# Two of the first four row tiles loaded on the ScalarE DMA queue instead of the SyncE queue

## The chip, the cores and the metric

The kernel runs on one core of one Trainium2 chip. The metric is the device time of one execution in microseconds (us). A profile covers the span of one execution, which is about 1.8 us shorter than the timed value (831.1 against 832.94 us for the changed kernel). The granted clock is the share of its full clock that TensorE was given; its mean over a run is 1.00 unless a number is stated.

Some names that recur: TensorE does matmuls (PE in the profile) and loads their weights (PEld). VectorE is DVE, ScalarE is ACT, GpSimd is POOL. In this kernel SyncE (SP) does nothing but issue transfers. A `q` after an engine's name (SPq, ACTq) means its instruction sequencer, which also issues transfers. Both SyncE and ScalarE issue loads here, each on a queue of its own (q1 and q10 in the profiles: 9.48 and 0.53 MB in the first 30 us of the changed kernel).

## The reference, cut to what matters

One transformer block: a layernorm with modulation, linear attention, a residual, a second layernorm, a gated feed-forward part. Only its beginning matters here:

```python
x = A_x                                            # 2048 x 1024, bfloat16
mod = (_silu(c) @ w_mod).reshape(c.shape[0], 6, 1, -1)
sa, ca, ga, sb, cb, gb = ...                       # six rows of 1024
h = _layernorm(x, axis=-1) * (1 + ca) + sa
q, k, v = split(h @ wqkv)                          # attention follows
```

The rows of `x` are taken in 16 tiles of 128 rows; four tiles make a chunk of 512 rows. Apart from one small transpose of `c`, TensorE can do nothing that the result needs before the first tiles have been loaded, normalized and transposed.

## The kernel before: the parts that the change touches

The kernel writes down all operations of all engines in one order; each engine executes its own in that order, and a wait is inserted wherever one operation needs another's result. The transfers at the start (cut):

```python
P.dma("c", CS8[0:NDT, :], cv8, queue="act")              # ScalarE queue
for st in range(4):                                       # row tiles 0..3, 256 KB each
    P.dma("x0_%d" % st, XRES[:, st, :], xv[:, st, :])     # SyncE queue
ca_load(0)            # w_mod, 1 MB, rows of 1 KB      (first weight load)
wq_load(0, 2)         # wqkv, 512 KB, rows of 2 KB
ca_load(1); wq_load(2, 2); ...                            # more weights, in order of use
```

The layernorm of the first chunk (cut; `dve`, `act`, `pe`, `pool` say which engine):

```python
warm(13, bank=3)                # PE: matmuls on zeros, to fill the time
act_stats(1)                    # ACT: mean and variance of tile 1, two passes
for f in s0_: f()               # DVE: statistics of tile 0
ln1_rstd1(0)                    # DVE + POOL: rstd, the scale of tile 0
s2_[0](); s2_[1]()              # DVE: statistics of tile 2
act_xn(0, MV[:, 0, 0:1])        # DVE: shift of tile 0 (nmr); ACT: normalizes tile 0
tile_transposes(0)              # PE: 8 transposes of tile 0
warm(5, bank=3)                 # PE
act_var(1)                      # DVE: from ACT's sums of tile 1
s2_[2]() ...                    # DVE, POOL: rstd of tiles 1 and 2
s3_[0](); s3_[1](); s3_[2]()    # DVE: statistics of tile 3
ln1_rstd1(3)
act_xn(1, SUMX[:, 1:2])         # DVE, ACT: normalizes tile 1
ln1_xn(2)                       # DVE: normalizes tile 2
tile_transposes(2)              # PE: 8 transposes of tile 2
mod_sc(WCA, 8, range(2))        # PE: first use of the first weight load
ln1_xn(3)                       # DVE: normalizes tile 3
tile_transposes(1, 3)           # PE
```

ScalarE normalizes tile 0 only after its own two passes over tile 1.

## Time and profile before

| | before |
|---|---|
| time, median of 6 runs (lowest to highest) | 831.07 us (830.88 to 831.25) |
| TensorE busy | 824.0 of 829.4 us |
| last landing event of tiles 0, 1, 2, 3 | 3.62, 4.25, 5.92, 6.58 us |
| first transposes (tile 0), then those of tile 2 | 8.76, 10.29 us |

A landing event is an increment of a load's semaphore in the trace; each of these loads has 16, and whoever waits for the load goes on after the last (tile 2's last comes at 5.92, and VectorE, which waits for it, starts at 5.94).

First the head of the page of the kernel before:

```profile
span 829.4 us, 10017 instructions
PE 824.0 (99%) x4083; PEld 378.4 (46%) x4083; DVE 312.0 (38%) x665; ACT 197.6 (24%) x336; POOL 39.8 (5%) x57
```

TensorE is busy nearly all the time, so only what delays TensorE counts. The chain that ended last, in order of time (columns: start, duration, what):

```profile
1.71 4.21 DMA xres<-in_A_x_dram
5.92 0.02 issue
5.94 1.29 DVE stats L176 x2
...
7.47 1.23 ACT xres L176
8.71 0.05 issue
8.76 818.08 PE ps L176 x4069
```

It reads: the load of tile 2 lands at 5.92, VectorE takes its statistics, then tile 0's shift; ScalarE normalizes tile 0; from 8.76 us to the end TensorE never waits. What happens on VectorE and on TensorE in between, from the timeline of the kernel before (start, duration, engine, source line, operation, output<-input, and in brackets the idle time before it and what ended that):

```profile
5.94 1.29 DVE L176 BATCH_NORM_STATS2 stats<-xres 128x6 f32<-128x512 bf16 x2 [0.58 <-DMA xres<-in_A_x_dram]
7.14 0.20 DVE L176 TENSOR_SCALAR nmr<-mv,rstd 128x1 f32<-128x1 f32 x1
7.88 1.27 DVE L176 BATCH_NORM_STATS2 stats<-xres 128x6 f32<-128x512 bf16 x2
9.62 1.18 DVE L176 TENSOR_SCALAR xres<-xres,mv,rstd 128x1024 bf16<-128x1024 bf16 x2
...
8.76 0.62 PE L176 MATMUL ps<-ident,xres 128*128 128x128 bf16 x8 [0.42 <-ACT xres L176]
9.21 1.24 PE L176 MATMUL ps<-e,ident 128*128 128x512 bf16 x5
10.29 0.61 PE L176 MATMUL ps<-ident,xres 128*128 128x128 bf16 x8
```

The statistics at 5.94 are tile 2's, those at 7.88 are tile 3's, and the normalization at 9.62 is tile 2's (its partner in the same line is tile 3's). On TensorE five fill matmuls stand between the transposes of tile 0 and those of tile 2. They are done at about 10.3 (matmuls overlap at their ends, so 9.21 + 1.24 reaches past 10.29), just after VectorE has finished the first half of its 1.18 us, tile 2 (about 10.2): the join is tight but without a wait.

### The profile page before, as it was taken

What the parts mean: (1) busy time and instruction counts of PE and PEld (TensorE: products, weight loads), DVE (VectorE), ACT (ScalarE), POOL (GpSimd) and SP (SyncE); (2) the same over time, 40 slices, a digit from 0 to 9 for tenths busy, and PEclk for the clock granted to TensorE, in tenths of its full rate; (3) what the DMA queues carried; (4) which work ended last, traced back from release to release, by engine and by line L of the source; (5) the groups of instructions that cost most, each with busy time, mean ns of one, the idle gap of its engine ahead of it and who ended that gap; (6) DMA issues with size and microseconds to landing.
All of it is one profiled execution on the core that took longest, in us unless ns stands there. A gap on an engine that the chain in (4) does not pass through costs nothing.

```text
span 829.4 us, 10017 instructions
## 1 busy us (share of the span) xinstructions
PE 824.0 (99%) x4083; PEld 378.4 (46%) x4083; DVE 312.0 (38%) x665; ACT 197.6 (24%) x336; POOL 39.8 (5%) x57
## 2 busy tenths in 40 slices
PE   8999999999999999999999999999999999999998
PEld 4544444454444444444444444444444444444444
DVE  5797986756955521121221111122111111221111
ACT  4757641323242111011111101111110111111011
POOL 1010000000130000030000003000000300000000
PEclk9999999999999999999999999999999999999999
DMA  9969655928397996700455570045557004553000
GB/s 320 288 151 229 149 159 172 202 102 304 60 258 225 259 267 174 192 25 14 128 150 155 150 188 28 15 126 153 153 153 187 26 18 125 154 151 86 0 26 26
DMA packets 199245, 119.28 MB, mean 144 GB/s; under 512 B 57880, under 2 KB 182944, under 8 KB 199200
## 3 DMA queue, kind: packets, MB, share of 16 engines
q1 hardware_dynamic: 199184, 118.65, 52.7%
q8 instruction: 32, 0.52, 0.3%
q14 instruction: 13, 0.11, 0.0%
q10 hardware_dynamic: 16, 0.00, 0.0%
HBM read 100.67 MB, written 4.33 MB: 127 GB/s over the span
## 4 chain that ended last, share of the span: by engine, by line
PE 99%; DMA 1%; DVE 0%; ACT 0%; SPq 0%; issue 0%
PE ps L176 99%; DMA xres<-in_A_x_dram 1%; DVE stats L176 0%; ACT xres L176 0%; SPq L176 0%; DVE xres L176 0%; DVE mv L176 0%; DVE nmr L176 0%
## 5 line engine op out<-in xcount | busy, mean ns | idle before, releaser
L176 PE MATMUL ps<-h2t,gug 128*128 128x512 bf16 x896 | 211.7, 379 | 0.0
L176 PE MATMUL ps<-h2t,guu 128*128 128x512 bf16 x896 | 211.7, 379 | 0.0
L176 DVE TENSOR_TENSOR at<-sg,ps 128x512 bf16<-128x512 bf16 x112 | 77.1, 688 | 282.7 <-PE ps L176 281.1
L176 ACT ACTIVATE sg<-ps 128x512 bf16<-128x512 f32 x112 | 66.9, 597 | 309.7 <-PE ps L176 309.7
L176 PEld LDWEIGHTS ps<-h2t,guu 128*128 128x128 bf16 x896 | 87.5, 98 | 105.8
L176 PEld LDWEIGHTS ps<-h2t,gug 128*128 128x128 bf16 x896 | 87.4, 98 | 105.7
L176 PE MATMUL ps<-wd_a,at 128*128 128x512 bf16 (+1 forms) x512 | 112.4, 378 | 0.0
L176 PE MATMUL ps<-ht,wqk 128*128 128x512 bf16 x512 | 111.7, 379 | 0.0
L176 PE MATMUL ps<-wd_b,at 128*128 128x512 bf16 (+1 forms) x384 | 85.0, 378 | 0.0
L176 PEld LDWEIGHTS ps<-wd_a,at 128*128 128x128 bf16 x512 | 50.0, 98 | 59.8
L176 DVE TENSOR_TENSOR ut<-att,gb_b 128x512 bf16<-128x512 bf16 (+1 forms) x32 | 13.8, 430 | 167.5 <-ACT att L176 167.5
L176 PEld LDWEIGHTS ps<-ht,wqk 128*128 128x128 bf16 x512 | 49.4, 98 | 58.8
L176 ACT ACTIVATE att<-ps 128x512 bf16<-128x512 f32 (+1 forms) x32 | 17.4, 591 | 182.1 <-PE ps L176 182.1
L176 PEld LDWEIGHTS ps<-wd_b,at 128*128 128x128 bf16 x384 | 37.5, 98 | 44.7
L176 PE MATMUL ps<-pk,xres 128*128 128x512 bf16 x256 | 56.5, 379 | 0.0
L176 PE MATMUL ps<-mw,pqt 128*128 128x512 bf16 x256 | 56.3, 379 | 0.0
L176 POOL TENSOR_SCALAR h2t<-h2t,modcol 128x512 bf16<-128x512 bf16 x32 | 26.4, 841 | 383.0 <-DMA h2t<-xn 383.0
L176 ACT ACTIVATE e<-ps 128x512 bf16<-128x512 f32 x56 | 33.1, 603 | 31.7 <-PE ps L176 20.5
L176 PEld LDWEIGHTS ps<-mw,pqt 128*128 128x128 bf16 x256 | 24.8, 98 | 30.3 <-DVE xres L176 0.4
L176 PEld LDWEIGHTS ps<-pk,xres 128*128 128x128 bf16 x256 | 24.8, 98 | 30.0 <-issue 0.4
L176 ACT ACTIVATE junk<-xres 128x1024 bf16<-128x1024 bf16 x24 | 25.4, 1058 | 35.1 <-DVE xres L176 34.9
L176 DVE SCALAR_TENSOR_TENSOR xres<-ps,xres 128x512 bf16<-128x512 f32 x32 | 21.4, 689 | 12.3 <-PE ps L176 11.7
(107 smaller groups left out, 346.0 us busy)
## 6 DMA issues: line engine op xcount, KB each, us to landing
gug<-in_B_w_gate_dram SPq DMA_DIRECT2D x56, 512.0 KB, 3.9
guu<-in_B_w_up_dram SPq DMA_DIRECT2D x56, 512.0 KB, 5.2
xres<-in_A_x_dram SPq DMA_DIRECT2D x20, 256.0 KB, 7.8
rb<-recip_den SPq DMA_DIRECT2D x8, 512.0 KB, 11.5
stgx<-in_w_mod_dram SPq DMA_DIRECT2D x2, 2048.0 KB, 7.8
wd_a<-in_B_w_down_dram SPq DMA_DIRECT2D x4, 1024.0 KB, 7.8
out_dram<-xres SPq DMA_DIRECT2D x31, 128.0 KB, 1.7
xres<-in_A_x_dram SPq DMA_DIRECT2D x3, 1024.0 KB, 14.0
```

What stands on the lines that cost most here:

```text
L176: return getattr(e, method)(**kw)
```

## The change

Its intent is to issue the four loads from two engines, so that the tiles are issued sooner and the weights behind them too.

```diff
         for st in range(4):
-            P.dma("x0_%d" % st, XRES[:, st, :], xv[:, st, :])
+            P.dma("x0_%d" % st, XRES[:, st, :], xv[:, st, :], queue="act" if st % 2 else "sp")
```

## The prediction

> **What bounds the kernel.** The page's first part has TensorE busy 824.0 of 829.4 us (99%). The chain of waits puts one unbroken run of 4,069 matmuls from 8.76 us to the end, 818.08 us; the waits view shows no matmul wait after 8.76 us. The granted clock is 1.00. So only the start of the first real transposes (8.76 us) moves the time, one for one, unless a later load comes late.
>
> The chain before 8.76 us (timeline): SyncE issues the row tiles at 0.79, 1.25, 1.71 and 2.18 us (0.40 to 0.43 us each). Their last landing events are at 3.62, 4.25, 5.92 and 6.58 us. VectorE takes tile 0's statistics at 3.64, waits for tile 2 (0.58 us idle), takes its statistics 5.94 to 7.22, and only then, in order, makes tile 0's shift (7.14 to 7.34). ScalarE normalizes tile 0 at 7.46 (1.24 us); TensorE follows at 8.76. So tile 2's landing sets the start.
>
> **What the change removes, adds, moves.** No work is added or removed.
> - Two issues leave SyncE: tile 2 is issued at about 1.25 instead of 1.71 us, the weight loads behind it 0.93 us sooner.
> - ScalarE gets two issues (about 0.43 us each) behind its load of c (0.79 to 1.37). Tile 1 is issued at about 1.40 (before: 1.25), tile 3 at about 1.86 (before: 2.18). ScalarE's table load moves from 1.40 to about 2.33, so SiLU of c ends near 3.8 and VectorE's copy of it near 4.0. Tile 0's statistics stand behind that copy: near 4.0 instead of 3.64.
> - [...] 365 and 389 GB/s from 2.5 to 3.5 us already. [...] Then tile 0 lands near 3.9, tile 1 near 4.5, tile 2 between 5.4 and 6.3, tile 3 near 6.7. No trace here shows two loaded queues yet.
>
> **Sum.** If tile 2 lands by 5.7, VectorE does 4.0 + 1.3 + 0.4 and goes on without a wait; transposes start near 8.55 (gain 0.2 us). If sharing holds tile 2 to 6.2, they start near 9.05 (loss 0.3 us). ScalarE's statistics of tile 1 (2.3 us) end by 6.9. The first weight load (landed 10.45, used 10.74) ends behind the same bytes and should hardly move. Expected: 831.2 us, 8 in 10 between 830.6 and 831.8. Faster by over 2% 0.003, within 2% 0.99, slower by over 2% 0.007.
>
> **What would show each step.** Timeline: ScalarE's three issues in a row, the table load near 2.33, tile 0's statistics near 4.0; idle of VectorE before tile 2's statistics tells whether sharing or VectorE binds. The chain: matmuls from 8.5 to 9.1 us, still about 818 us long. DMA view: two data queues, same bytes.
>
> **What would make it wrong.** With uneven sharing tile 2 could land near 5.0 or wait behind tiles 1 and 3 (loss up to 0.7 us). If the first weight loads are held back past their use near 10.7 or 12.4 us, TensorE stalls within the run of matmuls. [...] (first weight tile: median landing 8.78, last 10.45); if that lag changes, so do the landings.

## The result, and the profile after

The changed kernel took 832.32 us (median of 6 runs, 831.32 to 834.99) against 831.07. The ratio is 1.0019, with a 95% interval of 1.0005 to 1.0033. Ratios here are the mean time of one kernel's fast runs over that of the other's in the same rounds, so not quite the ratio of the medians. The class "within 2%" was right, which says little about a change of this size; the time is 0.5 us above the predicted range, and the scatter is 3.7 us where these six runs of the kernel before have 0.4 us. (On the four chips of the experiments the kernel before itself spread over 0.7 to 2.5 us.)

The page of the changed kernel:

```profile
span 831.1 us, 10017 instructions
PE 823.8 (99%) x4083; PEld 379.1 (46%) x4083; DVE 311.8 (38%) x665; ACT 197.5 (24%) x336; POOL 39.8 (5%) x57
```

The work is the same; the 1.7 us by which this profiled execution is longer are idle time. Its chain:

```profile
1.80 7.77 DMA xres<-in_A_x_dram
9.57 0.02 issue
9.60 1.30 DVE stats L176 x2
...
11.44 0.46 DVE xres L176
11.90 0.05 issue
11.95 816.58 PE ps L176 x4056
```

The load that now sets the start is tile 3's: issued at 1.80, 0.4 us sooner than before, and landed at 9.57, 3 us later. The timeline of the changed kernel, ScalarE, then VectorE, then TensorE:

```profile
1.41 0.84 ACTq L176 DMA_DIRECT2D xres<-in_A_x_dram  x2
2.28 1.28 ACT L176 ACT_TABLE_LOAD   x1 [2.28 <-issue]
5.06 1.06 ACT L176 ACTIVATE ht<-xres 128x1024 bf16<-128x1024 bf16 x1 [1.31 <-DMA xres<-in_A_x_dram]
7.30 1.22 ACT L176 ACTIVATE xres<-xres,nmr,rstd 128x1024 bf16<-128x1024 bf16 x1
...
6.68 0.20 DVE L176 TENSOR_SCALAR nmr<-mv,rstd 128x1 f32<-128x1 f32 x1
7.43 0.22 DVE L176 SCALAR_TENSOR_TENSOR mv<-sumx,sumsq 128x1 f32<-128x1 f32 x1 [0.55 <-ACT ht L176]
9.60 1.29 DVE L176 BATCH_NORM_STATS2 stats<-xres 128x6 f32<-128x512 bf16 x2 [1.46 <-DMA xres<-in_A_x_dram]
11.36 1.18 DVE L176 TENSOR_SCALAR xres<-xres,mv,rstd 128x1024 bf16<-128x1024 bf16 x2
...
8.58 0.62 PE L176 MATMUL ps<-ident,xres 128*128 128x128 bf16 x8 [0.66 <-ACT xres L176]
9.04 1.24 PE L176 MATMUL ps<-e,ident 128*128 128x512 bf16 x5
11.95 0.62 PE L176 MATMUL ps<-ident,xres 128*128 128x128 bf16 x8 [1.67 <-DVE xres L176]
```

Read from the bottom: the first transposes came at 8.58 instead of 8.76. (That is no shown gain: all profiles of the kernel before, two of them with a later load moved, have 8.42 to 8.82, and the three others of the changed start have 8.62 to 8.80.) Then TensorE ran out of fill matmuls and waited 1.67 us for tile 2, because VectorE was waiting 1.46 us for tile 3 in front of tile 2's normalization. From tile 2's transposes on both kernels take the same time: 829.4 - 10.29 = 819.11 us before and 831.1 - 11.95 = 819.15 us after. So in these two profiles the whole difference is made by 12 us.

Higher up, ScalarE begins with tile 1 at 5.06 (4.27 before), and VectorE waits 0.55 us for its sums. Tile 2 is no longer waited for; it landed at 4.36.

Why is tile 3 late? The DMA view of the changed kernel by queue, from 4.75 to 5.5 us and then from 5.5 to 8 us (q1 is SyncE's queue, q10 ScalarE's; packets, MB, share of 16 engines):

```profile
q1 hardware_dynamic: 237, 0.24, 105.3%
q10 hardware_dynamic: 1, 0.00, 0.7%
...
q1 hardware_dynamic: 697, 0.71, 81.0%
q10 hardware_dynamic: 135, 0.25, 25.8%
```

After tile 1 was done, the first weight load on SyncE's queue got all but one of 238 packets; only then did tile 3 get its share, about one packet in six (a quarter of the bytes, since its packets are larger: 1.9 KB on average against 1.0, from the packets and MB above). The first weight load was issued at 1.70, 0.1 us before tile 3.

One part of the lateness is of another kind. Half of tile 3's 16 landing events had come by 7.76 (5.82 before) and 15 by 8.52; the last came 1.06 us after the 15th. Had it come with the 15th, the transposes of tile 2 would have come near 10.9 instead of 11.95 (an estimate: 8.52 plus the 2.4 us that they took after the landing). So about 1 us of the wait of 1.67 us hangs on one late event. No view shows why it was late.

### The profile page after: what moved, and what is told of

Read it like the earlier page. It is cut to its first block, busy times and chain, and to the rows that moved or that the text cites. A ratio compares the mean times of both kernels' runs of the same rounds, so it can differ in the third digit from the quotient of the medians.

```text
span 831.1 us, 10017 instructions
## 1 busy us (share of the span) xinstructions
PE 823.8 (99%) x4083; PEld 379.1 (46%) x4083; DVE 311.8 (38%) x665; ACT 197.5 (24%) x336; POOL 39.8 (5%) x57
## 4 chain that ended last, share of the span: by engine, by line
PE 98%; DMA 1%; DVE 0%; ACTq 0%; issue 0%
PE ps L176 98%; DMA xres<-in_A_x_dram 1%; DVE stats L176 0%; ACTq L176 0%; DVE xres L176 0%; DVE mv L176 0%; DVE ve L176 0%; DVE nmr L176 0%
## 5 line engine op out<-in xcount | busy, mean ns | idle before, releaser
L176 ACT ACTIVATE att<-ps 128x512 bf16<-128x512 f32 (+1 forms) x32 | 17.4, 591 | 182.1 <-PE ps L176 182.1
```

The lines of the kernel that those rows point to most:

```text
L176: return getattr(e, method)(**kw)
```

## The experiments

Theory: tile 3 is held up by the weight loads on the other queue, and VectorE's order passes this on to tile 2. Rivals: the second queue as such is slow; VectorE's order alone is the cause; ScalarE's delayed table load or tile 1's later landing costs the time; the loss is made elsewhere in the kernel. (The table load has no run of its own. In the changed kernel's timeline it is not on the path: VectorE had tile 0's shift ready at 6.88, while ScalarE was busy with tile 1 until 7.40.) Each run was timed five times beside the kernel before on the same chip, four kernels to a chip.

| run | us, median | kernel before, same chip | ratio, 95% interval | tile 1 landed | tile 3 landed | tile 2's transposes |
|---|---|---|---|---|---|---|
| before | 831.07 | | | 4.25 | 6.58 | 10.29 |
| changed | 832.32 | 831.07 | 1.0019 (1.0005 to 1.0033) | 5.04 | 9.57 | 11.95 |
| e1 tile 1 only | 831.35 | 831.29 | 1.0001 (0.9988 to 1.0013) | 5.16 | 5.89 | 10.51 |
| e2 tile 3 only | 831.67 | 831.29 | 1.0008 (0.9995 to 1.0022) | 4.89 | 5.60 | 10.66 |
| e3 order swapped | 836.93 | 831.29 | 1.0070 (1.0057 to 1.0082) | 8.38 | 5.04 | 14.88 |
| e4 weights wait | 832.77 | 831.29 | 1.0019 (1.0006 to 1.0031) | 5.14 | 5.76 | 10.50 |
| e5 tile 4 first | 831.96 | 831.12 | 1.0010 (0.9997 to 1.0022) | 5.01 | 7.48 | 10.37 |
| e6 VectorE order | 832.75 | 831.12 | 1.0022 (1.0008 to 1.0035) | 5.23 | 8.39 | 10.31 |
| e7 tile 2 only | 831.76 | 831.12 | 1.0006 (0.9993 to 1.0018) | 4.58 | 5.94 | 9.94 |
| e8 changed again | 831.87 | 831.12 | 1.0008 (0.9995 to 1.0020) | 5.26 | 8.35 | 10.72 |
| e9 before again | 831.26 | 831.38 | 0.9994 (0.9981 to 1.0006) | 4.26 | 6.78 | 9.96 |
| e10 before, wo late | 831.19 | 831.38 | 0.9994 (0.9980 to 1.0008) | 4.20 | 6.58 | 10.03 |
| e11 changed, wo late | 831.84 | 831.38 | 1.0004 (0.9991 to 1.0016) | 5.23 | 7.83 | 10.59 |
| e12 tile 2, wo late | 831.09 | 831.38 | 0.9993 (0.9980 to 1.0005) | 5.11 | 6.38 | 10.57 |
| e13 before, wo late | 831.68 | 831.65 | 1.0002 (0.9988 to 1.0015) | 4.24 | 6.65 | 10.35 |
| e14 tile 1, wo late | 831.36 | 831.65 | 0.9998 (0.9986 to 1.0011) | 5.04 | 5.74 | 10.40 |
| e15 tile 3, wo late | 831.37 | 831.65 | 0.9999 (0.9987 to 1.0012) | 4.53 | 5.24 | 10.29 |
| e16 changed, wo late | 831.82 | 831.65 | 1.0005 (0.9993 to 1.0018) | 5.09 | 8.91 | 11.29 |

Landings and transposes are of the one profiled execution of each run; the medians are over five (six in the first two rows). Besides the changed kernel's first measurement, only the intervals of e3, e4 and e6 lie clear of 1. All runs gave correct results.

### e1: only tile 1 on the ScalarE queue

```diff
-  xv[:, st, :])
+  xv[:, st, :], queue="act" if st == 1 else "sp")
```

> Only tile 1 is loaded on the ScalarE queue; tile 3 goes back to SyncE, ahead of the first weight load. Theory (the changed kernel loses its time because the load of tile 3, on the other queue, is carried out beside the weight loads and lands at 9.57 instead of 6.58 us): tile 3 lands near 5.5 to 6, the wait before tile 2's transposes (1.7 us in the changed kernel) is gone, the first transposes stay near 8.6 and the time is 830.9 (830.6 to 831.2), at or just under the kernel before. Rival (any use of the second queue at the start costs, through ScalarE's delayed table load or through sharing): 831.8 or more.

Tile 3, back in front of the weights, landed at 5.89, and the long wait was gone: 831.35 against 831.29. The theory's mechanism held; its time (830.6 to 831.2) was too hopeful, and the rival's (831.8 or more) was not met. In this profile tile 2's transposes came at 10.51, because VectorE waited for ScalarE's sums of tile 1:

```profile
7.54 0.22 DVE L176 SCALAR_TENSOR_TENSOR mv<-sumx,sumsq 128x1 f32<-128x1 f32 x1 [0.95 <-ACT ht L176]
```

### e2: only tile 3 on the ScalarE queue

```diff
+  xv[:, st, :], queue="act" if st == 3 else "sp")
```

> Only tile 3 is loaded on the ScalarE queue, now as its first large load, issued at about 1.40 and so before the first weight load (about 2.2 us). Theory A (what counts is to be queued behind or beside the weight loads, not the tile or the queue): tile 3 lands near 5 as tile 1 did in the changed kernel, tile 2 near 5.7, time 831.0 (830.7 to 831.4). Rival B (as long as SyncE's queue has work, the ScalarE queue gets little): tile 3 lands after 7.5 again and the time is 832.0 to 832.8, as in the changed kernel.

Tile 3, now issued before the weights, landed at 5.60, so the queue as such does not make a load late, and neither does tile 3. Rival B's landing is refuted. The time, 831.67, is over theory A's range: tile 2, with tile 3 under way beside it, landed at 6.29 instead of 5.7.

### e3: the two ScalarE loads in the other order

```diff
-        for st in range(4):
+        for st in (0, 3, 2, 1):
             P.dma(..., queue="act" if st % 2 else "sp")
```

> As the changed kernel, but ScalarE issues tile 3 first and tile 1 second. Theory A (the second load on that queue is the late one, whichever tile it is): tile 3 lands near 5.0, tile 1 between 7.5 and 9.7; ScalarE then takes tile 1's statistics (2.2 us) from there and normalizes tile 0 only after it, so the first transposes move from 8.6 to between 11 and 13.2 us and the time is 833.5 to 835.6. Rival (tile 3's own rows are slow to read): tile 3 late again, tile 1 near 4.5 to 5, time as the changed kernel, 832.3.

The lateness moved with the position: tile 3 landed at 5.04, tile 1 at 8.38. The time, 836.93, is 1.3 us over the upper end expected. TensorE's timeline shows the extra:

```profile
11.92 1.04 PE L176 MATMUL ps<-ident,xres 128*128 128x128 bf16 x8 [4.09 <-ACT xres L176]
12.75 2.34 PE L176 MATMUL ps<-e,ident 128*128 128x512 bf16 x5
```

The same eight transposes took 0.62 us in the changed kernel, the same five fill matmuls 1.24. A row of the windows view of this run (us; busy time of PE, PEld, DVE, ACT, POOL; then granted clock, DMA share, GB/s) gives the cause, a clock of one half:

```profile
13.00:14.00 1.00, 1.00 (x3) 0.30 (x2) 0.91 (x4) 0.68 (x1) 0.56 (x1) 0.50 1.07 389
```

The same view has a mean clock of 0.82 from 8 to 12 us, 0.50 in every stretch from 12 to 17, 0.79 from 17 to 18 and 1.00 from 18 to 20. So the clock was halved near 10.6 us and came back near 17.4 (estimates from the 0.82 and the 0.79: full clock on one side, half on the other). The fall lies within the idle time of 4.09 us, about 2.7 us after the last matmul had ended (11.92 - 4.09 = 7.83). Idle times of 1.67 us (changed kernel) and 1.87 us (e13) did not halve it: the mean clock of both runs is 1.00. How long an idle time it takes is not shown. A halved clock may also be what stretched the changed kernel's slowest run (834.99 us, mean clock 0.998), of which there is no trace; that stays a guess. About 3.3 us at half clock would give such a mean and cost up to 1.7 us (an estimate: 0.002 of the span of 833.2 us is 1.7 us of lost clock; for e3, with a mean of 0.996, 0.004 of 835.0 us is 3.3 us, and its windows sum to 3.4). A run of e2 (833.33) and one of the kernel before (833.58, on the chip of e9) have the same 0.998, and the changed kernel's other five runs have 1.00, so only its largest outlier, and not its whole loss, can come from there.

### e4: the weights wait until tile 3 has landed

```diff
-            P.dma("x0_%d" % st, ...)
+            x0 = P.dma("x0_%d" % st, ..., queue="act" if st % 2 else "sp")
+        P.wait_for("sp", [x0])
```

> As the changed kernel, but SyncE waits for tile 3 to land before it issues the first weight load, so that nothing else is under way beside tile 3. Theory (the weight loads delay tile 3): tile 3 lands at 5.5 to 6.0 instead of 9.57, the wait before tile 2's transposes is gone; the weights start about 4 us later, so TensorE waits for them instead, and the time is 831.5 to 833.5. Rival (a second load on the ScalarE queue is slow in itself[...]): tile 3 still lands after 7.5 and all is later still, over 834.

This is the decisive run. With the same two loads on the ScalarE queue at the same moments and no weights beside them, tile 3 landed at 5.76 instead of 9.57, and tile 2's transposes came at 10.50, without the long wait:

```profile
9.14 1.24 PE L176 MATMUL ps<-e,ident 128*128 128x512 bf16 x5
10.50 0.62 PE L176 MATMUL ps<-ident,xres 128*128 128x128 bf16 x8
```

The rival is refuted: a second load on that queue is not slow in itself. The time was still 832.77, since the weights were now late. The waits view of this run has, for TensorE after 8 us:

```profile
PE ps L176 <- DMA wsa<-in_w_mod_dram: 0.7, 1, 0.7
PE ps L176 <- DVE g L176: 0.5, 1, 0.5
```

The first line is a weight load, as expected. The second is a wait that neither profile of the case had; more on it under e8.

### e5: one more row tile in front of the weights

```diff
+        P.dma("x1_0", XRES[:, 4, :], xv[:, 4, :])     # moved up from further down
         ca_load(0)
```

> As the changed kernel, but SyncE issues one more row tile (tile 4, 256 KB, needed only later) between tile 2 and the first weight load, so that tile 3 (issued at about 1.80) is issued before the first weight load (about 2.17) and its 256 KB competitor is tile 4. Theory D (loads of the two queues are served about in the order of issue; tile 3 was late because it was issued 0.1 us after the 1 MB weight load): tile 3 lands between 6.0 and 6.8 and the time is 831.2 to 831.7. Theory A (the SyncE queue takes long turns while it has work, whatever the order of issue): tile 3 lands after 7.2 and the time is 832 or more.

Fourteen of the 16 landing events of tile 3 came by 6.36, as theory D had them; the last two came at 7.20 and 7.48, as theory A had them. So most of tile 3 no longer waits through the weight load once it is issued before it, but two stragglers set the landing. The rule by which the queues share is not settled by this. The time, 831.96, is again blurred by the wait near 146 us (0.6 us in this profile).

### e6: VectorE normalizes tile 2 before it takes tile 3's statistics

```diff
-        s3_[0](); s3_[1](); s3_[2]()
-        ln1_rstd1(3)
         act_xn(1, SUMX[:, 1:2])
         ln1_xn(2)
+        s3_[0](); s3_[1](); s3_[2]()
+        ln1_rstd1(3)
```

> As the changed kernel, but on VectorE tile 3's statistics come after the normalization of tile 2, so that tile 2 no longer stands behind tile 3's landing. Theory (tile 3's late landing is the cause; the in-order VectorE only carries it): the wait of 1.7 us before tile 2's transposes goes away and comes back before the transposes of tiles 1 and 3, which need tile 3 normalized; net gain 0.2 to 0.5 us, time 831.8 to 832.2. Rival (the order on VectorE is the cause): the whole 1.5 us comes back, time 830.9 or less.

The wait moved to where the theory had it, to the transposes of tiles 1 and 3. TensorE's timeline:

```profile
10.31 0.61 PE L176 MATMUL ps<-ident,xres 128*128 128x128 bf16 x8
10.75 0.54 PE L176 MATMUL ps<-siluc,wca 128*128 128x1 bf16 x16
11.16 0.22 PE L176 MATMUL ps<-ident,xres 128*128 128x128 bf16 x1
12.71 1.01 PE L176 MATMUL ps<-ident,xres 128*128 128x128 bf16 x15 [1.34 <-DVE xres L176]
```

But nothing was gained: 832.75, when the unmodified changed kernel took 831.87 on this chip (e8). The expected gain of 0.2 to 0.5 us was a miss. Where tile 3 landed at 8.39, VectorE could have begun with it then; here it began at 9.73, after a wait for GpSimd's part of tile 2. So the rival's forecast, that a better order on VectorE brings the whole loss back (830.9 or less), failed. But this run does not show that its own wait comes from tile 3's landing: the new order brought a wait of its own. The order does carry the delay to tile 2, as the first profile shows.

### e7: only tile 2 on the ScalarE queue

```diff
+  xv[:, st, :], queue="act" if st == 2 else "sp")
```

> Only tile 2 is loaded on the ScalarE queue; tiles 0, 1 and 3 on SyncE in front of the weights. From the runs so far: tile 1 lands near 4.4, tile 2 near 5.1, tile 3 near 5.8; ScalarE's statistics of tile 1 end near 6.7 (7.4 where tile 1 was on the ScalarE queue), VectorE has tile 0's shift by 6.6, so the first transposes start near 8.0 and tile 2's near 9.7 (10.29 before). If nothing later takes it back, 830.6 (830.3 to 831.0), better than both kernels. If the first weight loads then bind (landing 8.9 to 10.5, used near 10.1), about 831.0 and a wait of TensorE on a weight load shows.

In the profiled run the start is the earliest of all, tile 0's transposes at 8.12 and tile 2's at 9.94. That is not yet a gain by the change: the kernel before has 9.96 in e9, and the same start has 10.57 in e12. The time did not gain: 831.76 against 831.12, a miss. The profiled run was the fastest of the five (831.30); TensorE lost 0.4 us near 146 us in it, 0.2 us of which shows as a wait. The other four runs have no profile. This run asked for the wait near 146 us to be removed, which e10 to e16 do.

### e8: the changed kernel again

No edit.

> The changed kernel itself again, on the same chip as the other three. Theory (its time follows tile 3's landing, which differs from run to run): 831.5 to 833 with a wider range than the kernel before, over 1 us; tile 3 lands after 7 in the profiled run and the wait before tile 2's transposes is tile 3's landing minus about 7.9 us, as in the first profile (9.57 to 1.67).

The time was 831.87 (831.41 to 832.67). Tile 3 landed at 8.35. The relation to its landing that was expected (a wait of about 0.45 us) failed: tile 2's transposes came at 10.72 and the wait before them was only 0.2 us. Yet the span was 830.9 us, 1.5 us over the kernel before. Following the starts of TensorE's weight loads one by one against the kernel before, the difference is 0.5 us from tile 2's transposes to 146 us and 1.5 us from there on. The timeline there:

```profile
142.83 3.83 PE L176 MATMUL ps<-pk,xres 128*128 128x512 bf16 x17
147.49 2.76 PE L176 MATMUL ps<-pk,xres 128*128 128x512 bf16 x11 [0.83 <-DVE g L176]
```

A matmul waits for a bank of PSUM (the memory that matmuls write to) that VectorE must empty, and VectorE waits, through ScalarE, for a bias that is broadcast through two small transfers. In SyncE's order these stand behind a 2 MB load of `wo`. They landed at 141.5 and 145.8 here, at 140.0 and 143.7 in the kernel before. So there are two places where this kernel can lose about a microsecond.

The two do not simply add up. In all eleven profiles with `wo` at its old place, what TensorE loses at 146 us is the landing of the second small transfer minus 144.37 us minus the delay that TensorE already has by then against the kernel before, where that is above zero: 145.85 - 144.37 - 0.48 = 1.00 us here. In the changed kernel's first profile that transfer landed just as late, at 145.80, but the start's delay of 1.70 us hid it; in the kernel before there were 0.69 us to spare. Whether the change makes the second wait likelier is open: it shows in four of the nine profiles with a load on the ScalarE queue (e4, e5, e7, e8) and in neither of the two of the kernel before (the first and e9).

### e9, e10, e11, e12: the second wait taken away

e9 is the kernel before itself. The other three issue the load of `wo` after the two small transfers:

```diff
-        P.dma("wo", WO[:], wov)
         G_BANKS = ...
 ...
             if g == 0:
                 z_row()                    # the two small transfers
+                P.dma("wo", WO[:], wov)
```

e10 does this to the kernel before, e11 to the changed kernel, e12 to e7.

> The kernel before itself, as a control on the chip of the next three. In the profiles so far some runs have a second wait of TensorE, near 146 us, for the bias that VectorE and ScalarE make from the broadcast sum of the keys (its two small transfers stand behind the 2 MB load of wo): none before, none in the changed kernel's first profile, 1.0 us in its second. Theory (that wait comes and goes with transfer times, in the kernel before too): time 830.7 to 832, the four tiles land by 6.7, the transposes of tile 2 are at 10.1 to 10.4 and a second wait of 0 to 1 us may show. Rival (only kernels with loads on ScalarE have it): no second wait, 831.0 to 831.3.

> The kernel before, with the 2 MB load of wo issued after the two small transfers of the key sum instead of in front of them. If those transfers were late because of that load, they land about 5 us sooner (first one in 2 to 3 us instead of 7.4), the second wait cannot occur, and the time is 830.7 to 831.2 with a narrow range. If wo then comes too late for its own use near 158 us, slower than 832.

> The changed kernel with the same late load of wo: what remains against the kernel before with late wo is the start alone. Theory (tile 3's lateness and tile 1's later statistics cost 0.3 to 1.7 us at the start): 831.2 to 832.8, and 0.3 to 1.7 us more than the kernel before with late wo; no second wait near 146 us; the whole difference of the two profiles is there by tile 2's transposes. Rival (the change costs in the middle of the kernel): no difference between the two.

> Only tile 2 on the ScalarE queue, and the late load of wo. The start gained 0.3 us in the profile of that kernel and a second wait of 0.4 us took it back. Without that wait: 830.4 to 830.9, about 0.3 us under the kernel before with late wo, and faster than both kernels of the case, by under 0.1%. If it is not, the start's gain is within the scatter of the runs.

e9 had no second wait in its profile and took 831.26, which is what the rival had (only kernels with loads on ScalarE have that wait); one profile does not decide it. The other runs of the kernel before on that chip went up to 833.58, so it has bad runs too, but what caused them was not traced. In e10 the first small transfer took 2.7 us instead of 7.4, the second landed at 137.8 instead of 143.7, and the time was 831.19 with a narrow range (830.98 to 831.36). In e11 there was no second wait either, and the time was 831.84, 0.65 us over e10 by the medians. The two profiled runs differ by 0.57 us (831.55 against 830.98), all of it before tile 2's transposes (10.59 against 10.03, and no further difference to the end); in e11 these were held by tile 1 and not by tile 3. So the change can lose time at the start alone, which the rival, a loss in the middle of the kernel only, did not have; with `wo` early e8 had both. e12 took 831.09, 0.1 us under e10 and within the scatter; its 830.4 to 830.9 was a miss. No version was found that beats the kernel before clearly.

### e13 to e16: how the loss splits

All four with `wo` late: the kernel before, tile 1 only, tile 3 only, and the changed kernel.

> Kernel before with late wo, again, as the base of the next three on this chip: 831.2 (830.9 to 831.5), tile 2's transposes at 9.9 to 10.3, no second wait.

> Only tile 1 on the ScalarE queue, with late wo. Theory (tile 1 lands 0.8 to 1.0 us later there, ScalarE ends its statistics at 7.3 to 7.5 instead of 6.6, and VectorE's work for tiles 1 and 2 waits for them): 0.2 to 0.4 us over the base; tile 2's transposes at 10.3 to 10.7. Rival (all of the loss is tile 3): within 0.1 us of the base.

> Only tile 3 on the ScalarE queue, with late wo. It is issued before the weights there, lands near 5.6 and takes its share from tile 2 (6.3): 0.2 to 0.6 us over the base, by tile 2's statistics on VectorE, not by tile 3's.

> The changed kernel with late wo, again. Theory (tile 1's part, 0.2 to 0.4 us, in every run, and on top what tile 3 lands later than about 8 us): 0.5 to 1.2 us over the base, wider scatter than the other three. If tile 3 lands before 8 us in the profiled run, tile 2's transposes are at 10.4 to 10.8; if later, at about its landing plus 2.4 us.

The base came out slower and wider than expected (831.68, 831.19 to 832.20; its profile loses 0.4 us between 15 and 50 us, which no run explains), so the differences in time are small: e14 -0.3, e15 -0.3, e16 +0.1 us. The expected 0.2 to 0.4 us for tile 1 alone, 0.2 to 0.6 us for tile 3 alone and 0.5 to 1.2 us for the changed kernel are misses; all three are within the scatter of the base. So these times do not split the loss. What did stand out is e14's scatter: 831.32 to 831.41. Its start does not hang on tile 2, which lands at 4.37 and is needed at 5.06, but on tile 1, which landed at about the same moment in e1 and e14; that this is the reason is not shown. The changed kernel was nominally the slowest of the four here too, with tile 2's transposes at 11.29:

```profile
8.93 1.29 DVE L176 BATCH_NORM_STATS2 stats<-xres 128x6 f32<-128x512 bf16 x2 [0.75 <-DMA xres<-in_A_x_dram]
11.29 0.62 PE L176 MATMUL ps<-ident,xres 128*128 128x128 bf16 x8 [0.96 <-DVE xres L176]
```

Now the profiles with the changed start can be put side by side. From tile 3's landing to tile 2's transposes it is 11.95 - 9.57 = 2.38 us in the first, 11.29 - 8.91 = 2.38 in e16, 10.72 - 8.35 = 2.37 in e8. In e11 and e5 tile 3 landed at 7.83 and 7.48, VectorE was not yet free, and the transposes came at 10.59 and 10.37, set by tile 1 as in e1 (10.51) and e14 (10.40). So in these five profiles the start is the later of two things: about 10.4 to 10.6 us, set by tile 1, or tile 3's landing plus 2.4 us. The kernel before has 9.96 to 10.35 in its four profiles (two of them with late `wo`).

## Why the prediction was wrong

- **"So only the start of the first real transposes (8.76 us) moves the time, one for one, unless a later load comes late".** This is the step that failed. The chain of the kernel before was taken as proof that everything after 8.76 us is safe; the exception at the end was worked out for tile 2 and the weight loads, not for tile 3. The join at tile 2's transposes had almost no slack: the fill matmuls ended just after tile 2 was ready. The changed kernel started its first transposes at 8.58, where the prediction had 8.55, and then lost 1.67 us inside what had been one run of matmuls. That 8.58 is so near to 8.55 is luck: VectorE, which was to set it, had tile 0's shift ready at 6.88, and ScalarE's statistics of tile 1, which were not to matter, held tile 0 until 7.30; the three other profiles of the changed start have 8.62 to 8.80.
- **"Tile 3 near 6.7".** The term of the sum that was mis-sized. It landed at 9.57 in the first profile and at 7.83 to 8.91 in the three other looks at the changed start (e8, e11, e16). It was the author's estimate, for an even sharing of tile 3 with the first weight load, which no trace had shown; the DMA view shows 1 packet of 238, then 135 of 832. e4 shows that the weight loads are the cause, e2 and e3 that it is the position behind them and not the tile or the queue. In the first profile 1.06 us of the lateness is one straggling landing event, of the kind that the prediction's last line warned of. The list of what would make it wrong did name tile 2 behind another load, up to 0.7 us, and weights held back, but not tile 3 behind the weights.
- **"ScalarE's statistics of tile 1 end by 6.9".** They ended at 7.40. Tile 1 landed at 5.04 instead of the 4.5 that was estimated. This took the slack out of tile 2's path even where tile 3 was in time (e1, e5, e14). Its part in the time is within the scatter (e14).
- **Right:** tile 2's landing is no longer what VectorE waits for (4.36, and its statistics at 5.49 without a wait); the table load at 2.28; tile 0's statistics at 3.86; the same work and bytes, carried by two queues; the first weight load came no later (9.84 against 10.44).
- **Not foreseen:** the scatter. Six runs of the changed kernel spread over 3.7 us. Its landing of tile 3 differs by 1.7 us between four looks, and a second wait near 146 us comes and goes with up to 1 us. By the medians the changed kernel is 0.65 and 0.14 us slower than the kernel before with `wo` late, on two chips, and 1.25 and 0.75 us with `wo` early; only the 1.25 us has an interval clear of zero. So the profiles show where the first profiled run lost its time; how much the change costs on average is known only roughly.

Left open: the rule by which the two queues share, whether the change makes the second wait likelier, and why in some runs a few of the 16 landing events of a load come 0.5 to 1.7 us after the others (the 1.7 in the first weight load of the kernel before: median 8.77, last 10.44).

## What to carry to other kernels

Here a load moved to a second queue was no longer ahead of what the first queue issued next (it landed at 9.57 instead of 6.58 us, issued 0.1 us behind a load of 1 MB): ask which large load will be under way when it wants to move, and keep what is needed first in front of the bulk, on the same queue (tile 3 landed at 5.89 in e1) or issued clearly earlier (5.60 in e2). A chain of waits without gaps shows no slack at the joins; before predicting a gain at its head, find for each later join what arrives there and how much earlier than needed. And where a kernel has two independent places that can lose a microsecond at random, take one away before measuring an effect of that size in the other; a delay at the first can also hide a wait at the second.
